# Attention stage of a fused attention, MoE and MLP kernel: router tables in the steps without a conversion, a 16-bit sign operation, local values loaded ready-made, value copies on ScalarE

## The chip, the cores and the metric

The kernel runs on one core of a Trainium2 chip. The metric is the device time of one execution in microseconds, as the median of three runs. The engines are named as in the profile: PE (TensorE matmul), PEld (its weight loads), DVE (VectorE), ACT (ScalarE), POOL (GpSimd), SP (SyncE, which issues the loads and stores here). L12 means line 12 of the kernel before; where the changed kernel is meant, the text says so.

## What is computed

Three layers follow one another. Only the first is touched by the change, apart from tables that the second needs.

```python
def _attn_ref(q, k, v, n_global, n_local):          # (4, 8, 768, 64), 8 global, 96 local
    scores = scale * np.matmul(q, k.transpose(0, 1, 3, 2))
    keep = is_global | is_local                     # 8 first columns, or 96 last ones
    scores = np.where(keep, scores + bias, -1e9)
    a = softmax(scores)
    return np.matmul(a, v)

x = _moe_ref(x, w_gate, w1, w2)                     # 3072 tokens, 8 experts, capacity 384, greedy by logit
return _moe2_ref(x, w_in, w_out, alpha)             # float64 weights w_in, w_out; parametric ReLU
```

The softmax weights, the values and x are fp32. `w_in` and `w_out` arrive as 64-bit floats and are turned into fp32 on the chip, during the attention stage.

## The kernel before

**Attention, lines 90 to 340.** The 3072 rows are 24 tiles of 128 queries (4 batches of 6 tiles, `g`), and each tile is done in two half steps (`u`) of four heads. That makes 48 steps, counted by `n`; `steps[n]` is `(g, u)`. The engines each have a queue in program order, and the order of the code in the loop over `n` is therefore the order of work on each of them. In step `n` the loop issues, in turn: the loads for later tiles (SP), `scores` of step n+1 (eight matmuls on PE, L193; four minimum-and-add operations on DVE, L199, into `a_sx`; four exponentials on ACT, L202, into `a_p`), `transpose_p` of step n (PE, L213; the own block's copy `a_pts0` on DVE, L217; the block of earlier keys `a_pts1` on ACT, L215), `divisor` (POOL, L243), `combine` of step n-2 (PE L261; DVE L247, L270, L280 and at u = 1 L283), and `values` of step n-1 (PE, L232; the copy `a_xt` out of PSUM, L236 on ACT at u = 1 and L238 on DVE at u = 0).

**Values of earlier keys.** A tile that is not the first of its batch looks at 96 local keys of the tile before and at 8 global keys. The kernel before takes them from the tile before as it stands: `place_values` (L173, copy in L177 on POOL) overwrites the first 32 rows of that tile's values with a strip `a_vg`, in which the global values lie beside zeros, once the tile before has used them. The weights `a_p` are 256 columns wide, with zeros in front.

**Conversion of the 64-bit weights, `Doubles`, lines 30 to 87.** There are 32 jobs of 128x512 numbers. In a step with `turn(n)` (`2 <= n < 45` and `n % 5 < 4`, so four steps of five, called turn steps here) one job begins and is joined: `begin` runs two ACT operations (L72, L74) and one on POOL (L73), before the step's scores; `join` runs at the step's end two operations on DVE (L78 shifts, L79 puts the sign bit in) and one on POOL (L81). `finish` of every second job runs two more on POOL (L86, L87) in the next turn step. The raw numbers `f_raw` have three buffers, so the load of job k is issued when L81 of job k-3 is over.

**Router tables, `Router.setup`, from line 465.** Constants for the MoE routing are made by small operations on POOL and DVE. `setup` is a generator that the attention loop steps once in each step from n = 1, whether it is a turn step or not.

After the attention stage comes the routing, whose first search runs with nothing beside it, and then the experts' matmuls, one expert after the other, with the rest of the routing among them.

```python
if turn(n):
    next(side)
if n:
    next(setup, None)
```

## Time and profile before

| | us |
|---|---|
| median of three runs (lowest, highest) | 1077.29 (1076.77, 1078.17) |
| the profiled execution | 1076.5 |
| its span, first to last instruction | 1074.7 |
| busy in the span: PE, DVE, ACT, POOL | 1032.3, 739.1, 380.3, 559.5 |
| mean granted TensorE clock | 0.986 of full speed |

The attention stage is the first 196 us or so of the span; the rest is routing and the experts. The profile's page cuts the span into 40 slices of 26.9 us. The views by stretch, by group, by wait and by time are asked for the attention stage alone, since an average over the whole span says little on it.

### The profile page before, as it was taken

What the parts mean: (1) busy time and instruction counts of PE and PEld (TensorE: products, weight loads), DVE (VectorE), ACT (ScalarE), POOL (GpSimd) and SP (SyncE); (2) the same over time, 40 slices, a digit from 0 to 9 for tenths busy, and PEclk for the clock granted to TensorE, in tenths of its full rate; (3) what the DMA queues carried; (4) which work ended last, traced back from release to release, by engine and by line L of the source; (5) the groups of instructions that cost most, each with busy time, mean ns of one, the idle gap of its engine ahead of it and who ended that gap; (6) DMA issues with size and microseconds to landing.
All of it is one profiled execution on the core that took longest, in us unless ns stands there. A gap on an engine that the chain in (4) does not pass through costs nothing.

```text
span 1074.7 us, 19352 instructions
## 1 busy us (share of the span) xinstructions
PE 1032.3 (96%) x6475; PEld 908.8 (85%) x6475; DVE 739.1 (69%) x2215; ACT 380.3 (35%) x958; POOL 559.5 (52%) x867
## 2 busy tenths in 40 slices
PE   8888989789999999999999999999999999999997
PEld 6766767569888988898899888988998999999996
DVE  7999999787878787877887788678855313231322
ACT  6788878233224311331233123312321232124211
POOL 5867876055668434643564346433742464247223
PEclk9999999799999999999999999999999999999999
DMA  8677774152254336335433643543354335335141
GB/s 287 221 243 262 269 268 156 31 150 77 98 193 151 127 109 215 99 109 175 157 93 106 208 136 98 163 151 119 99 175 139 120 124 189 118 118 167 60 136 70
DMA packets 86771, 160.80 MB, mean 150 GB/s; under 512 B 9584, under 2 KB 42864, under 8 KB 86672
## 3 DMA queue, kind: packets, MB, share of 16 engines
q1 hardware_dynamic: 82832, 146.98, 41.3%
q0 software_dynamic: 3840, 12.59, 3.5%
q8 instruction: 51, 0.84, 0.3%
q14 instruction: 48, 0.39, 0.1%
HBM read 138.57 MB, written 20.97 MB: 148 GB/s over the span
## 4 chain that ended last, share of the span: by engine, by line
PE 74%; DVE 6%; POOL 3%; issue 3%; DMA 1%; ACT 1%; POOLq 0%; DVEq 0%; ACTq 0%
PE m_h L983 22%; PE m_acc L1028 22%; PE m_acc L970 12%; PE m_h L943 11%; POOL m_g L912 1%; PE a_xp L232 1%; PE a_pt L213 1%; POOL m_so L912 1%; PE a_s L193 1%; DMA m_x<-x_rows,r_idx 1%; PE m_h L869 1%; ACT a_p L202 1%; DVE r_red L795 1%; PE a_cb L261 1%; DVE a_sx L199 1%
## 5 line engine op out<-in xcount | busy, mean ns | idle before, releaser
L912 POOL TENSOR_TENSOR m_g<-m_t,m_g 128x192 fp32r<-128x192 f32 (+1 forms) x286 | 163.7, 594 | 335.6 <-ACT m_g L992 335.0
L1028 PE MATMUL m_acc<-m_so,m_g 128*128 128x512 f32 x1143 | 294.0, 398 | 0.0
L983 PE MATMUL m_h<-m_y,wi 128*128 128x384 f32 x1536 | 290.1, 339 | 0.0
L983 PEld LDWEIGHTS m_h<-m_y,wi 128*128 128x128 f32 x1536 | 267.4, 188 | 6.6 <-DVE m_xt L885 0.2
L1028 PEld LDWEIGHTS m_acc<-m_so,m_g 128*128 128x128 f32 x1143 | 209.2, 189 | 34.5 <-POOL m_g L912 0.5
L912 POOL TENSOR_TENSOR m_s<-m_r,m_s 128x256 fp32r<-128x256 f32 x256 | 187.3, 755 | 77.5 <-ACT m_s L902 77.2
L992 ACT ACTIVATE m_g<-m_t 128x384 fp32r<-128x384 f32 (+1 forms) x143 | 70.0, 489 | 427.0 <-DVE m_t L991 249.1
L990 DVE TENSOR_SCALAR m_t<-m_h,m_al 128x384 f32<-128x384 f32 (+1 forms) x144 | 82.3, 571 | 155.7 <-PE m_h L983 145.4
L970 PE MATMUL m_acc<-m_hh,m_s 128*128 128x384 f32 x768 | 148.0, 339 | 0.0
L943 PE MATMUL m_h<-m_xt,m_s 128*128 128x384 f32 x768 | 144.4, 336 | 0.6 <-DVE m_xt L885 0.4
L943 PEld LDWEIGHTS m_h<-m_xt,m_s 128*128 128x128 f32 x768 | 134.5, 188 | 2.4 <-DVE m_xt L885 0.6
L970 PEld LDWEIGHTS m_acc<-m_hh,m_s 128*128 128x128 f32 x768 | 132.7, 189 | 0.0
L902 ACT ACTIVATE m_s<-m_r 128x512 fp32r<-128x512 f32 x128 | 79.7, 626 | 68.4 <-PE m_acc L970 66.7
L202 ACT ACTIVATE a_p<-a_sx,a_mn 128x232 f32<-128x232 f32 (+1 forms) x192 | 88.4, 462 | 38.2 <-DVE a_mn L199 38.2
L947 DVE SCALAR_TENSOR_TENSOR m_hh<-m_h,m_hh 128x384 fp32r<-128x384 f32 x64 | 35.5, 555 | 78.4 <-ACT m_hh L946 78.2
L991 DVE SCALAR_TENSOR_TENSOR m_t<-m_h,m_t 128x384 f32<-128x384 f32 (+1 forms) x144 | 73.9, 513 | 4.9
L795 DVE TENSOR_REDUCE r_red<-r_cmp 128x24 bf16<-128x576 bf16 (+1 forms) x97 | 73.8, 761 | 3.3
L213 PE MATMUL a_pt<-ident,a_p 128*128 128x128 f32 x352 | 57.3, 294 | 15.9 <-DVE a_r L247 13.2
L213 PEld LDWEIGHTS a_pt<-ident,a_p 128*128 128x128 f32 x352 | 39.2, 144 | 36.9 <-ACT a_p L202 23.1
L199 DVE CUSTOM_DVE_ANT_0 a_sx<-a_s,a_bias 128x232 f32<-128x232 f32 (+1 forms) x192 | 61.4, 374 | 4.3 <-PE a_s L193 2.6
L946 ACT ACTIVATE m_hh<-m_h 128x384 fp32r<-128x384 f32 x64 | 31.5, 492 | 91.1 <-PE m_h L943 88.8
L193 PE MATMUL a_s<-a_k,a_q 64*128 64x232 f32 (+1 forms) x384 | 51.0, 388 | 3.6 <-DMA a_q<-in_q_dram 3.6
(192 smaller groups left out, 1162.4 us busy)
## 6 DMA issues: line engine op xcount, KB each, us to landing
m_so<-wo_pairs SPq DMA_DIRECT2D x112, 512.0 KB, 3.5
m_r<-in_moe_w_dram SPq DMA_DIRECT2D x128, 256.0 KB, 3.0
a_k<-in_k_dram SPq DMA_DIRECT2D x20, 464.0 KB, 5.2
f_raw<-in_moe_w_in_dram SPq DMA_DIRECT2D x16, 512.0 KB, 4.0
f_raw<-in_moe_w_out_dram SPq DMA_DIRECT2D x16, 512.0 KB, 5.4
wo_pairs<-m_so SPq DMA_DIRECT2D x16, 512.0 KB, 2.7
a_v<-in_v_dram SPq DMA_DIRECT2D x24, 256.0 KB, 5.1
x_rows<-a_xo SPq DMA_DIRECT2D x24, 256.0 KB, 3.0
```

The source lines that it names most:

```text
L199: nc.vector.tensor_tensor_reduce(out=sx[:, s, :n], in0=ps[s][:, a, :n], in1=bs[:, h], scale=-scale, scalar=BIG, op0=OP.add, op1=OP.min, ac ...
L202: nc.scalar.activation(pr[:, s, 2 * C - n:], sx[:, s, :n], AF.Exp, bias=T["mn", g][:, h:h + 1], scale=-1.0, accum_out=T["sum", g][:, h:h + 1])
L213: nc.tensor.transpose(ps[:, i], pr[:, :C] if part else pr[:, C:], ident)
L795: nc.vector.tensor_reduce(red, cmp, axis=AX.X, op=OP.add)
L902: self.nc.scalar.activation(s[:, 0], r, AF.Copy)
L912: self.nc.gpsimd.tensor_tensor(lo[:, c:c + n], x[:, c:c + n], hi[:, c:c + n], op=OP.subtract)
L943: nc.tensor.matmul(ps[:, :n], s1[:, a, d], x[:, b, d], start=(d == 0 and i == 0), stop=(d == self.ND - 1 and i == 2))
L970: nc.tensor.matmul(ps[:, :n], s2[:, b, d * 128:(d + 1) * 128], h[:, a], start=(f == 0 and a + b == 0), stop=(last and a == 1))
L983: nc.tensor.matmul(ps[:, :n], self.wi[:, a, d, f * 128:(f + 1) * 128], y[:, b, d], start=(d == 0 and i == 0), stop=(d == self.ND - 1 and i ...
L990: nc.vector.tensor_scalar(t[:, cs], ps[:, cs], 0.0, self.al[:, f:f + 1], op0=OP.min, op1=OP.mult)
L991: nc.vector.scalar_tensor_tensor(t[:, cs], ps[:, cs], 0.0, t[:, cs], op0=OP.max, op1=OP.add)
L1028: self.nc.tensor.matmul(self.ex[e]["op"][t], g[:, a, t * 128:(t + 1) * 128], s[:, b], start=(f == 0 and a + b == 0), stop=(f == self.F2 // ...
```

## The change

Five edits, all in the attention stage:

1. `join` no longer puts the sign into the shifted number. It masks the top 16 bits of the high word and writes them into the top 16 bits of the low word's place, which are zero there, and the addition on POOL (L81) then carries the sign along. The operation has one input instead of two, of 16-bit elements that lie 8 bytes apart.
2. The local and global values of earlier keys are laid out in DRAM as an input `vw` of 104 rows per tile, and loaded as a tile `a_vw` with a DMA of its own (20 in all, 104 x 2 KB). `place_values`, `a_vg` and its loads, and two memsets go. `a_v` has three buffers instead of four.
3. The weights are 232 instead of 256 columns wide, and the block of earlier keys is transposed as 104 rows.
4. `a_xt` is copied on ACT in every step.
5. `setup` is stepped only in steps that are not turn steps, and its pieces are cut anew; the two copies that make `r_tp` go from DVE to ACT.

```diff
     def join(self, job):
         nc, t = self.nc, job["t"]
+        parts = job["raw"].bitcast(U16).rearrange("p a (b c) -> p a b c", c=2)
         nc.vector.tensor_scalar(t, t, 3, 0x7FFFFFF8, op0=OP.logical_shift_left, op1=OP.bitwise_and)
-        nc.vector.scalar_tensor_tensor(t, job["raw"][:, :, 1], -0x80000000, t, op0=OP.bitwise_and, op1=OP.bitwise_or)
+        nc.vector.tensor_scalar(parts[:, :, 0, 1], parts[:, :, 1, 1], 0x8000, None, op0=OP.bitwise_and)
...
-        x = T["v", g] = loads.tile([C, H, D], FT, name="a_v", bufs=4)
+        x = T["v", g] = loads.tile([C, H, D], FT, name="a_v", bufs=3)
         nc.sync.dma_start(x, v[b, t * C:(t + 1) * C])
-        if not t:
-            nc.sync.dma_start(vg[C - GW:C - W, b % 2], v[b, :G])
+        if t:
+            x = T["vw", g] = loads.tile([GW, H, D], FT, name="a_vw", bufs=3)
+            nc.sync.dma_start(x, vw[b, t - 1])
...
-    def place_values(g, u):
-        b, t = divmod(g, NT)
-        if t:
-            hs = slice(4 * u, 4 * u + 4)
-            nc.gpsimd.tensor_copy(T["v", g - 1][:C - W, hs], vg[:, b % 2, hs])
...
+        m = GW if part else C
+        ps = psum.tile([C, 4, C], FT, name=f"a_pt{part}")[:m]
+        sb = work.tile([C, 4, C], FT, name=f"a_pts{part}", bufs=2)[:m]
...
-            parts.append((T["v", g - 1], T.pop(("PT", g, u, 1))))
+            parts.append((T["vw", g], T.pop(("PT", g, u, 1))))
...
-        if u:
-            nc.scalar.activation(xt, ps, AF.Copy)
-        else:
-            nc.vector.tensor_copy(xt, ps)
+        nc.scalar.activation(xt, ps, AF.Copy)
...
-        if n + 1 < N:
-            place_values(*steps[n + 1])
         if turn(n):
             next(side)
-        if n:
+        else:
             next(setup, None)
...
-        nc.vector.tensor_copy(self.tp[:, :, 0], first[:, :, None].to_broadcast([128, U, NB, 2]))
-        nc.vector.tensor_copy(self.tp[:, :, 1], inner[:, :, None, None].to_broadcast([128, U, NB, 2]))
+        for k, t in enumerate((first[:, :, None], inner[:, :, None, None])):
+            nc.scalar.activation(self.tp[:, :, k], t.to_broadcast([128, U, NB, 2]), AF.Copy)
```

How the queues change, at three places. First DVE at the end of a turn step with odd n, before the change (`a_pts`, `a_lp`, `a_xo` and `logits` belong to transposition and combination, `f_t` and `f_raw` to the conversion):

```order
L217 COPY a_pts_484<-a_pt_483 128x512 [waits PE_49]
L247 RECIPROCAL a_r<-a_se 128x4 [waits Pool_49]
L270 TENSOR_TENSOR a_lp<-a_cb,a_r 128x32 [waits DVE_49,PE_49]
L280 TENSOR_TENSOR a_xo<-a_cb,a_r 128x256
L283 TENSOR_REDUCE logits<-a_lp 128x8 [waits DVE_49]
L238 COPY a_xt<-a_xp 128x256 [waits PE_49]
L78 TENSOR_SCALAR f_t<-f_t 128x512 [waits Pool_49]
L79 SCALAR_TENSOR_TENSOR f_t<-f_raw,f_t 128x512 [waits DMAHW1_49,DVE_49]
```

The same step in the changed kernel:

```order
L211 COPY a_pts_494<-a_pt_493 128x512 [waits PE_49]
L238 RECIPROCAL a_r<-a_se 128x4 [waits Pool_49]
L261 TENSOR_TENSOR a_lp<-a_cb,a_r 128x32 [waits DVE_49,PE_49]
L271 TENSOR_TENSOR a_xo<-a_cb,a_r 128x256
L274 TENSOR_REDUCE logits<-a_lp 128x8 [waits DVE_49]
L79 TENSOR_SCALAR f_t<-f_t 128x512 [waits Pool_49]
L80 TENSOR_SCALAR f_raw<-f_raw 128x512 [waits DMAHW2_49,Activation_49]
```

The copy of `a_xt` is gone from DVE, and the last operation waits for ACT (L74, which writes the low word's place) instead of for the operation in front of it.

Second, ACT over two turn steps, before:

```order
L202 ACTIVATE a_p,a_sum<-a_sx,a_mn 128x232 x4
L215 ACTIVATE a_pts_631<-a_pt_630 128x512
L72 ACTIVATE f_t<-f_raw 128x512
L74 ACTIVATE f_raw<-f_raw 128x512
L202 ACTIVATE a_p,a_sum<-a_sx,a_mn 128x232 x4
L215 ACTIVATE a_pts_702<-a_pt_701 128x512
L236 ACTIVATE a_xt<-a_xp 128x256
```

And after (each exponential stands in a row of its own there):

```order
L195 ACTIVATE a_p,a_sum<-a_sx,a_mn 128x232 [waits DVE_49,Activation_49]
L209 ACTIVATE a_pts_635<-a_pt_634 104x512 [waits PE_49,Activation_49]
L229 ACTIVATE a_xt<-a_xp 128x256 [waits PE_49,Activation_49]
L72 ACTIVATE f_t<-f_raw 128x512 [waits DMAHW7_49,Pool_49]
L74 ACTIVATE f_raw<-f_raw 128x512
...
L209 ACTIVATE a_pts_696<-a_pt_695 104x512 [waits PE_49,Activation_49]
L229 ACTIVATE a_xt<-a_xp 128x256 [waits PE_49,Activation_49]
```

Now every step has a copy of `a_xt` behind `a_pts` and ahead of the next conversion, and this copy waits for PE's `values`.

Third, POOL over a turn step in which a job is finished, before:

```order
L501 IOTA r_grid 128x52
L501 IOTA r_grid 128x46
L501 IOTA r_grid 128x50
L73 TENSOR_SCALAR f_t<-f_t 128x512
L86 TENSOR_SCALAR wi<-f_t 128x512
L87 TENSOR_TENSOR wi<-f_t,wi 128x512
L243 TENSOR_SCALAR a_se<-a_sum 128x4
L177 COPY a_v<-a_vg 32x256
L81 TENSOR_TENSOR wo<-f_t,f_raw 128x512
```

And after:

```order
L73 TENSOR_SCALAR f_t<-f_t 128x512
L87 TENSOR_SCALAR wi<-f_t 128x512
L88 TENSOR_TENSOR wi<-f_t,wi 128x512
L234 TENSOR_SCALAR a_se<-a_sum 128x4
L82 TENSOR_TENSOR wo<-f_t,f_raw 128x512
```

The tables and the copy into `a_v`, which waits for PE, no longer stand between the conversion's operations. The tables' POOL part stands in steps 0, 1 and 4.

## Rows read from the trace of the kernel before

**Rows 1.** The page, part 2: DVE's busy tenths in 40 slices of 26.9 us.

```profile
DVE  7999999787878787877887788678855313231322
```

**Rows 2.** Busy time by stretch: PE, PEld, DVE, ACT, POOL, granted clock, DMA share, GB/s.

```profile
0.00:20.00 20.00, 16.07 (x112) 11.94 (x112) 15.29 (x77) 11.93 (x44) 8.99 (x26) 1.00 0.85 286
20.00:180.00 160.00, 144.26 (x1344) 112.66 (x1343) 152.44 (x588) 132.22 (x430) 121.38 (x178) 0.97 0.74 249
180.00:200.00 20.00, 18.28 (x203) 14.78 (x201) 17.50 (x76) 12.89 (x48) 5.46 (x13) 1.00 0.12 43
```

**Rows 3.** Waits in 20 to 180 us: us in total, times, longest.

```profile
ACT a_p L202 <- DVE a_mn L199: 27.3, 25, 2.6
...
DVE a_sx L199 <- ACT f_raw L74: 0.7, 1, 0.7
...
DVE a_xt L238 <- PE a_xp L232: 0.4, 2, 0.2
```

**Rows 4.** The chain that ended last, pieces in order: start, length, what.

```profile
120.86 0.39 DVE a_sx L199
...
123.28 0.49 ACT a_pts L215
...
129.72 0.98 PE a_s L193 x8
...
133.24 0.98 PE a_s L193 x8
...
160.60 0.39 DVE a_sx L199
```

**Rows 5.** Timeline of DVE at a turn step's end, odd n: start, duration, instruction.

```profile
104.13 0.42 DVE L238 COPY a_xt<-a_xp 128x256 f32<-128x256 f32 x1
104.46 0.47 DVE L78 TENSOR_SCALAR f_t<-f_t 128x512 int32<-128x512 int32 x1
104.97 0.69 DVE L79 SCALAR_TENSOR_TENSOR f_t<-f_raw,f_t 128x512 int32<-128x512 int32 x1
105.57 0.28 DVE L199 CUSTOM_DVE_ANT_0 a_sx<-a_s,a_bias 128x128 f32<-128x128 f32 x1
```

**Rows 6.** Lines 78 and 79 on DVE: duration ns min/median/max, first and last start.

```profile
L78 DVE TENSOR_SCALAR f_t<-f_t x32: 415/430/1354, 19.9 to 179.0; 128x512 int32<-128x512 int32 x32
...
L79 DVE SCALAR_TENSOR_TENSOR f_t<-f_raw,f_t x32: 691/693/1651, 20.3 to 179.5; 128x512 int32<-128x512 int32 x32
```

**Rows 7.** Timeline of DVE and POOL where two operations meet.

```profile
100.00 1.33 POOL L87 TENSOR_TENSOR wi<-f_t,wi 128x512 fp32r<-128x512 f32 x1
100.23 1.65 DVE L79 SCALAR_TENSOR_TENSOR f_t<-f_raw,f_t 128x512 int32<-128x512 int32 x1
```

**Rows 8.** Timeline of ACT in a stretch without idle time.

```profile
107.46 0.36 ACT L236 ACTIVATE a_xt<-a_xp 128x256 f32<-128x256 f32 x1
107.72 0.66 ACT L72 ACTIVATE f_t<-f_raw 128x512 f32<-128x512 f32 x1
...
108.86 0.47 ACT L202 ACTIVATE a_p<-a_sx,a_mn 128x232 f32<-128x232 f32 x1
...
110.75 0.66 ACT L72 ACTIVATE f_t<-f_raw 128x512 f32<-128x512 f32 x1
```

**Rows 9.** Timeline of DVE: the longest operations of the router tables.

```profile
37.11 1.37 DVE L507 CAST r_tp<-r_first 128x288 bf16<-128x288 f32 x1
...
42.90 1.22 DVE L518 TENSOR_SCALAR r_mask<-r_rows 24x4 bf16<-24x4 int32 x1
...
51.28 1.65 DVE L529 TENSOR_SCALAR r_step<-r_digits 128x72 uint16<-128x72 f32 x2
```

**Rows 10.** Tile `f_raw`: L81's duration (ns min/median/max), and the loads' time to landing.

```profile
L81 POOL TENSOR_TENSOR f_t<-f_t,f_raw x16: 1272/1292/1307, 21.2 to 176.6; 128x512 int32<-128x512 int32 x16
...
DMA to landing us min/median/max: 3.8/4.9/8.2
```

**Rows 11.** Groups on POOL, 0 to 200 us: busy, mean ns, idle before it and its releaser.

```profile
L177 POOL COPY a_v<-a_vg 32x256 f32<-32x256 f32 x40 | 21.5, 538 | 16.6 <-PE a_xp L232 14.6
```

More of the change, by code (lines that the diff above doesn't have):

```diff
@@ L87, in finish, with attention @@
             self.nc.gpsimd.tensor_tensor(job["lo"], v, job["hi"], op=OP.subtract)
-def attention(ctx, tc, q, k0, k, v, w_gate, n_global, n_local, ident, x_dram, logits, side, router):
+def attention(ctx, tc, q, k0, k, v, vw, w_gate, n_global, n_local, ident, x_dram, logits, side, router):
     nc = tc.nc
@@ L208, in transpose_p @@
             return
-        ps = psum.tile([C, 4, C], FT, name=f"a_pt{part}")
-        sb = work.tile([C, 4, C], FT, name=f"a_pts{part}", bufs=2)
+        m = GW if part else C
+        ps = psum.tile([C, 4, C], FT, name=f"a_pt{part}")[:m]
+        sb = work.tile([C, 4, C], FT, name=f"a_pts{part}", bufs=2)[:m]
         for i in range(4):
             pr = T["P", g, 2 * u + i // 2][:, i % 2]
-            nc.tensor.transpose(ps[:, i], pr[:, :C] if part else pr[:, C:], ident)
+            nc.tensor.transpose(ps[:, i], pr[:, :GW] if part else pr[:, GW:], ident)
         if part:
@@ L489, in setup @@
         W, U = self.WIDE, TT // 2
+        ng = 128 // B
+        rows = 2 * NB
         self.slots = iota([128, B // W, TT, W], U16, "r_slots", [[W, B // W], [0, TT], [1, W]])
-        yield
         self.blocks = iota([128, U, NB, 2], U16, "r_blocks", [[0, U], [1, NB], [0, 2]])
-        yield
         first = iota([128, U, 2], FT, "r_first", [[256, U], [128, 2]])
@@ L496, in setup @@
         order = iota([128, E], FT, "r_order", [[-1, E]], base=E)
+        at = iota([rows, ng], I32, "r_rows", [[-1, ng]], base=ng, slope=1)
+        of = iota([rows, 2, NB // ng], I32, "r_cols", [[-NB, 2], [-ng, NB // ng]], base=rows, slope=1)
+        yield
         digits = iota([128, D, TT], FT, "r_digits", [[1, D], [0, TT]], base=1)
         self.last = iota([128, D + 1], FT, "r_last", [[1, D + 1]], base=1)
-        yield
         for (d, size), g in zip(self.HIGH + self.LOW, self.grids):
@@ L530, in setup @@
             self.steps.append(step)
-            if i % 2:
+            if i % 3 == 2:
                 yield
+        yield
         self.ahead = consts.tile([128, 2 * TT], FT, name="r_ahead")
@@ L1151 @@
     v: bass.AP,
+    vw: bass.AP,
     n_global: int,
@@ L1188 @@
         items = [item for both in zip(first, second) for item in both]
-        attention(actx, tc, q, k0, k, v, w_gate, n_global, n_local, ident, x_dram, logits, doubles.jobs(items), router)
+        attention(actx, tc, q, k0, k, v, vw, w_gate, n_global, n_local, ident, x_dram, logits, doubles.jobs(items), router)
         assert doubles.idle
@@ L1216, in _lay_out, with reach @@
     out["k0"] = pairs(k[:, :, None, :c])[:, 0]
-    out["k"] = pairs(np.stack([np.concatenate([k[:, :, :n_global], k[:, :, t * c - n_local:(t + 1) * c]], axis=2)
-                               for t in range(1, s // c)], axis=2))
+    def reach(x, end):
+        return np.stack([np.concatenate([x[:, :, :n_global], x[:, :, t * c - n_local:t * c + end]], axis=2)
+                         for t in range(1, s // c)], axis=2)
+    out["k"] = pairs(reach(k, c))
     out["v"] = inputs["v"].transpose(0, 2, 1, 3)
+    out["vw"] = reach(inputs["v"], 0).transpose(0, 2, 3, 1, 4)
     return out
```

15 lines of the change are left out of this document (3 added, 12 removed).

## The prediction

> **What bounds the kernel now.** I began with the page's busy tenths: DVE is near full in the first seven slices, the attention stage, and at seven to eight tenths after them [rows 1]. All edits lie in that stage, so I asked for busy time by stretch. From 20 to 180 us DVE is busy 152.44 of 160 us, PE 144.26, ACT 132.22 and POOL 121.38 [rows 2]. A busy PE is partly modelled, so I checked by the waits who is waiting: DVE has four entries in that stretch, from 0.7 to 0.4 us in total each, 2.2 us together, while ACT alone waits 27.3 us for DVE's minimum [rows 3]. DVE sets the pace; what it is spared is time, until another engine's queue is as long. What follows the stage depends on its end and is not edited, so it moves with it.
>
> The unit to count in is five steps, four turn steps with a conversion and one without. On the chain the first `a_sx` of a step starts on DVE at 120.86 and, ten steps later, at 160.60 [rows 4]: 39.74 us, **19.87 us per five steps**. The 32 jobs make eight such units.
>
> **What DVE is spared.** Operations on it overlap their neighbours a little, so I count from start to start.
>
> - Copy of `a_xt`: 104.46 - 104.13 = 0.33 us [rows 5]. It is on DVE in every second step, 2.5 per unit: 0.83 us. (The copies before the first and after the last job, 3 of 24, I count at nothing: DVE is not full there, 17.50 of 20 us in the last stretch [rows 2].)
> - Sign bit: L78 takes 0.43 us in the median and L79 0.69 [rows 6]. In rows 5 L78 is followed by L79 0.04 us after its end, since L79 reads what L78 writes, while L79's successor starts 0.09 before L79 ends. So the pair costs now 0.43 + 0.04 + 0.69 - 0.09 = 1.07 us. The new operation has one input in SBUF and 512 elements, as L78 has, and does not read L78's result. If it runs like L78, the pair costs 2 x (0.43 - 0.09) = 0.68 us and each turn step is spared 0.39, which I round to 0.36, for the odd spacing of its elements: 1.44 us per unit. The other bound is that it streams one element per tick as L79 does: 0.69, and then only the dependency is saved, 0.13 us per turn step, 0.26 less than at the first bound. No row has a 16-bit operation of this size. I take the value near L78, the row most alike in operands. The Trainium skill (VectorE: DVE Perf Modes, What auto-detection actually checks) would give it to the new operation on the same grounds: a single source and the destination in SBUF with even dimensions suffice for two elements a tick, and no spacing is asked for. L78's 415 ns, under the 533 ns of 512 ticks at the clock stated there, agrees for closely packed elements; no run here shows spaced ones.
> - Router tables: three entries of 1.37, 1.22 and 1.65 us [rows 9] stand at the end of turn steps, less 0.08 overlap each: 4.0 us in all. The first goes to ACT; the others go to steps without a conversion, which have room for them (below). The smaller ones I leave out.
>
> By DVE alone a unit would fall to 19.87 - 0.83 - 1.44 = **17.6 us**.
>
> **What the other engines allow.** PE: between two starts of `a_s` with no gap lie 133.24 - 129.72 = 3.52 us [rows 4], so five steps take at least 17.6 us. ACT: four exponentials take 110.75 - 108.86 = 1.89 us, the conversion's two operations 108.86 - 107.72 = 1.14, a copy of `a_xt` 107.72 - 107.46 = 0.26 [rows 8], `a_pts1` 0.49 [rows 4]. With the copy in every step a turn step has 3.78 us of ACT work and the fifth 2.64: 17.8 us per unit. So three queues of 17.6 to 17.8 us meet, in different rhythms: ACT is the longest in turn steps (3.78), PE in the fifth (3.52 against 2.64). Some of each rhythm is lost at the others. POOL has the room: it loses 40 copies, 21.5 us, and the 14.6 us in which it stood waiting for PE in front of them [rows 11]. But POOL and DVE go on getting in each other's way: beside a POOL operation that began 0.23 us earlier, L79 took 1.65 instead of 0.69 us [rows 7], and the longest L78 1.35 instead of 0.43 [rows 6]. These waits are in the 19.87 and I leave them in. I take **18.1 us** per unit, 0.3 above ACT's sum.
>
> **New waits.** The sign operation now waits for L74 on ACT, behind which all of DVE's next step is queued. L74 runs before the step's exponentials, some two microseconds ahead: nothing, and if the raw numbers came late, DVE would wait anyway for L78's input. The copy of `a_xt` on ACT waits for PE's `values`; the conversion and the next exponentials are queued behind it. At u = 1 it stands there already. SP gets 20 more issues, each with 104 x 2 KB = 213 KB, 4.3 MB in all, and is rid of four small ones. Some 18 of them fall between 20 and 180 us; that adds 3.8 MB in 160 us, 24 GB/s, to 249, and the shorter unit makes (249 + 24) x 19.87 / 18.1 = 300 of it; in proportion the DMA share goes from 0.74 to 0.89. The first 20 us ran 286 GB/s at 0.85 [rows 2], so this fits, with little to spare. Two of the new loads stand ahead of the first raw numbers: 0.5 us. Transposing 104 instead of 128 rows and the narrower weights change no column count on PE: nothing. The two memsets that go: nothing, since POOL was busy for only 8.99 of the first 20 us [rows 2].
>
> **The sum.** Eight units: 8 x (19.87 - 18.1) = 14.2 us. Tables: 4.0, of which 1.0 is lost because ACT's 3.78 us fill those steps instead: 3.0. First loads: -0.5. Together 16.7 us. The profiled execution took 1076.5 us (span 1074.7 and 1.8 around it), so 1059.8; the median of the three runs is 0.8 higher, so **1060.5 us**.
>
> **Rivals.**
>
> *A, the sign operation is no cheaper.* Either it streams one element per tick, or it loses its gain to POOL. The second is to be taken seriously: two operations of L78's kind then stand one behind the other, and a POOL operation that gets in between makes the second wait as in rows 7, at up to 0.96 us. The Trainium skill (SBUF — State Buffer, Who interferes with whom) has the rule: the two share a port pair, and who comes second waits for the whole instruction. Rows 7 agree. DVE's unit is then 17.6 + 4 x 0.26 = 18.64, with little lost at the others 18.84: 8 x 1.03 + 2.5 = 10.7 us gained, 1066.6 us. Chance 0.2.
>
> *B, the queues mesh and the POOL waits shrink*, as the copies into `a_v` no longer delay L81 and what follows. The unit falls to ACT's 17.8, and the tables count in full: 8 x 2.07 + 4.0 = 20.6 us, 1056.7 us; with PE's sum 1055. For it: ACT's 27.3 us of waiting show that it can run ahead. Against: nothing here has three full queues. Chance 0.15.
>
> *C, ACT becomes the gate.* If the copy of `a_xt` waits for PE's last work of a step in each step, the 1.14 us of the conversion come after it and no longer beside PE's work. Where half of it, 0.57 us in four steps, is lost on top of 17.8, the unit is 20.1, and only the tables are gained: 1077.3 - 2.5 + 1.8 = 1076.6 us. Against: the exponentials run a step ahead of their transposition, and at u = 1 the order is the same today without any such wait among the long ones. Chance 0.09.
>
> *D, slower: the raw numbers come late.* Load of job k starts when L81 of job k-3 ends. From the start of L72 to the end of L81 it is about one step, 3.97 us, L81's 1.29 [rows 10] and some 0.6 between: 5.9 us. Three jobs thus take at least landing + 5.9, a unit 4/3 of it. With the median landing of 4.9 us [rows 10] that is 14.4 us, no bound. It decides from a landing of 9.0 us on (19.87); today's longest is 8.2. At 11 us, where the fuller DMA engines would have to push it, the unit is 22.5: 8 x 2.66 - 2.5 = 19 us lost, 1096 us. For it: a share of 0.89. Against: the median is far off, and the loads issued per step are limited, so that no backlog builds up. Chance 0.06.
>
> **How the numbers follow.** The forecast has 0.5, with 1057 to 1064 for units of 17.8 to 18.5 us; A reaches to 1070 and B to 1053. 1053 to 1070 leaves out D, C and the ends of A and B, some 0.2. A measurement tells apart about 0.2%, 2.2 us. Faster: the forecast, A, B and the half of C in which less is lost at ACT, 0.9; within 0.2% the rest of C, 0.04; slower D, 0.06.
>
> **What would show it.** In the changed profile: the stage's last `a_xp` some 17 us earlier; 18.1 us per five steps; DVE's busy share from 20 to 160 us below 0.95 with waits for PE or ACT among its first; L80 near 0.43 us in the median; the 27.3 us in which ACT waits for DVE shrunk to under a third; DMA near 300 GB/s with landings under 7 us. A median of 0.69 for L80, or a sum of its waits above 8 us, means A; ACT's doubles waiting for a DMA means D. I am wrong in kind, not in size, if DVE is still without waits and the unit is above 19 us.

## The result, and the profile after

The changed kernel takes **1064.43 us** (median of five runs, 1063.83 to 1066.32) against 1076.77 us of the kernel before in five runs on the same chip: a ratio of 0.9885, 95% interval 0.9871 to 0.9898. So 12.3 us are gained, where 16.7 were forecast. The profiled execution took 1064.5 us, its span 1062.8. The gain lies in the attention stage: the last `a_xp` on PE starts at 184.3 us instead of 195.7, 11.4 us earlier where 17 were forecast, and what follows takes as long as before (878.5 against 879.0 us). From here on line numbers are those of the changed kernel: L79 is the shift, L80 the new sign operation, L82 the addition on POOL, L88 its subtraction in `finish`, L192 the score reduction, L195 the exponentials, L229 the copy `a_xt`.

Busy time by stretch, of the changed kernel: stretch, its length, PE, PEld, DVE, ACT, POOL with their instructions, granted clock, DMA share, GB/s [answers to rows 2].

```profile
0.00:20.00 20.00, 14.03 (x96) 10.74 (x98) 13.19 (x70) 10.81 (x39) 7.40 (x26) 1.00 0.90 289
20.00:160.00 140.00, 133.07 (x1280) 102.90 (x1276) 133.59 (x542) 129.88 (x432) 102.26 (x134) 1.00 0.90 298
20.00:180.00 160.00, 152.54 (x1467) 118.18 (x1464) 151.57 (x613) 146.76 (x490) 112.41 (x148) 1.00 0.84 278
```

ACT and PE have come up to DVE: from 20 to 160 us the three are busy 129.88, 133.07 and 133.59 of 140 us. DVE itself is about as busy as before: 151.57 of 160 us, where rows 2 have 152.44. The waits, 20 to 180 us: us in total, times, longest [answers to rows 3].

```profile
POOL f_t L82 <- DVE f_raw L80: 15.3, 12, 1.7
...
ACT a_p L195 <- DVE a_mn L192: 11.4, 15, 1.6
...
DVE a_sx L192 <- PE a_s L186: 2.7, 3, 1.2
...
DVE f_t L79 <- POOL f_t L73: 0.7, 1, 0.7
```

DVE waits 3.8 us in 160, in four entries of which the two longest are shown; that is about as little as before (2.2), so it is still the bound. What it does with its time is seen in the two operations of `join`: first the duration in ns (min/median/max) and first and last start, then the groups with busy time and mean ns, of the changed kernel [answers to rows 6].

```profile
L79 DVE TENSOR_SCALAR f_t<-f_t x32: 410/419/1355, 21.0 to 167.6; 128x512 int32<-128x512 int32 x32
...
L80 DVE TENSOR_SCALAR f_raw<-f_raw x32: 737/750/1835, 21.3 to 168.0; 128x512 uint16<-128x512 uint16 x32
...
L80 DVE TENSOR_SCALAR f_raw<-f_raw 128x512 uint16<-128x512 uint16 x32 | 34.0, 1064 | 0.0
...
L79 DVE TENSOR_SCALAR f_t<-f_t 128x512 int32<-128x512 int32 x32 | 16.5, 517 | 0.8 <-POOL f_t L73 0.7
```

The same groups of the kernel before, where L79 is the old sign operation and L78 the shift:

```profile
L79 DVE SCALAR_TENSOR_TENSOR f_t<-f_raw,f_t 128x512 int32<-128x512 int32 x32 | 26.6, 832 | 1.1
L78 DVE TENSOR_SCALAR f_t<-f_t 128x512 int32<-128x512 int32 x32 | 19.2, 599 | 0.6 <-POOL f_t L73 0.5
```

The new sign operation takes 0.750 us in the median, not 0.43, and not even the 0.693 of the old one [rows 6]; its mean is 1.064. The mean of the pair went up, from 599 + 832 = 1431 ns to 517 + 1064 = 1581. Two places on DVE's timeline show the two cases (start, duration, instruction):

```profile
110.69 0.42 DVE L79 TENSOR_SCALAR f_t<-f_t 128x512 int32<-128x512 int32 x1
111.02 1.82 DVE L80 TENSOR_SCALAR f_raw<-f_raw 128x512 uint16<-128x512 uint16 x1
112.64 0.41 DVE L192 CUSTOM_DVE_ANT_0 a_sx<-a_s,a_bias 128x232 f32<-128x232 f32 x1
...
115.25 0.42 DVE L79 TENSOR_SCALAR f_t<-f_t 128x512 int32<-128x512 int32 x1
115.58 0.75 DVE L80 TENSOR_SCALAR f_raw<-f_raw 128x512 uint16<-128x512 uint16 x1
116.11 0.42 DVE L192 CUSTOM_DVE_ANT_0 a_sx<-a_s,a_bias 128x232 f32<-128x232 f32 x1
...
150.51 0.42 DVE L192 CUSTOM_DVE_ANT_0 a_sx<-a_s,a_bias 128x232 f32<-128x232 f32 x1
```

And POOL's at the first of them:

```profile
110.84 1.40 POOL L88 TENSOR_TENSOR wi<-f_t,wi 128x512 fp32r<-128x512 f32 x1
```

Undisturbed, the pair costs 116.11 - 115.25 = 0.86 us from start to start, where the prediction had 1.07 before and 0.68 after: 0.21 us saved, not 0.36. L80, begun at 111.02, takes 1.82 us: POOL's L88, begun while L79 ran, is over at 112.24, and L80 ends 0.60 us after that. Nine of the 32 sign operations are of that kind, all in steps with a `finish`. One more (1.16 us) and four shifts (0.91 to 1.35 us) meet operations of a `finish` too, so that 14 of its 16 turns cost the pair time.

In the kernel before, 13 of 16 did, so the meetings are not more frequent now; they are longer. There POOL's subtraction (L87) had mostly begun ahead of the shift, which then lost only what was left of it:

```profile
118.66 1.27 POOL L87 TENSOR_TENSOR wi<-f_t,wi 128x512 fp32r<-128x512 f32 x1
118.88 1.33 DVE L78 TENSOR_SCALAR f_t<-f_t 128x512 int32<-128x512 int32 x1
120.25 0.69 DVE L79 SCALAR_TENSOR_TENSOR f_t<-f_raw,f_t 128x512 int32<-128x512 int32 x1
```

Of the subtractions that met the pair, eight began ahead of the shift before the change and four behind its start; in the changed kernel it is four and nine.

The unit of five steps comes from the first and the last L192 that end a pair there, ten steps apart (n = 28 to 38, as in rows 4): (150.51 - 112.64) / 2 = **18.93 us**, against 19.87 before and 18.1 forecast. From the first score reduction of step 13 to that of step 43 (52.11 to 164.94 us; before 56.78 to 176.40) it is 18.81 against 19.94. The loads of the raw numbers, tile `f_raw`, time to landing [answers to rows 10]:

```profile
DMA to landing us min/median/max: 5.0/7.8/8.0
```

### The profile page after: what moved, and what is told of

Its sections match the earlier page's. It is cut to its first block, busy times and chain, and to the rows that moved or that the text cites. A ratio compares the mean times of both kernels' runs of the same rounds, so it can differ in the third digit from the quotient of the medians.

```text
span 1062.8 us, 19360 instructions
## 1 busy us (share of the span) xinstructions
PE 1027.4 (97%) x6475; PEld 904.7 (85%) x6475; DVE 725.7 (68%) x2189; ACT 386.4 (36%) x984; POOL 544.0 (51%) x825
## 4 chain that ended last, share of the span: by engine, by line
PE 79%; DVE 8%; POOL 4%; issue 3%; ACT 3%; DMA 2%; SPq 0%; POOLq 0%; ACTq 0%; DVEq 0%
PE m_h L969 23%; PE m_acc L1014 23%; PE m_acc L956 12%; PE m_h L929 12%; PE a_pt L207 2%; PE a_xp L226 2%; PE a_s L186 2%; ACT a_p L195 2%; DVE f_raw L80 1%; POOL m_so L898 1%; POOL m_g L898 1%; PE a_cb L252 1%; DVE a_sx L192 1%; PE m_h L855 1%; DMA f_raw<-in_moe_w_out_dram 1%
## 5 line engine op out<-in xcount | busy, mean ns | idle before, releaser
L195 ACT ACTIVATE a_p<-a_sx,a_mn 128x232 f32<-128x232 f32 (+1 forms) x192 | 88.4, 466 | 19.5 <-DVE a_mn L192 19.3
L192 DVE CUSTOM_DVE_ANT_0 a_sx<-a_s,a_bias 128x232 f32<-128x232 f32 (+1 forms) x192 | 62.4, 381 | 7.2 <-PE a_s L186 7.0
L207 PE MATMUL a_pt<-ident,a_p 128*128 128x128 f32 (+1 forms) x352 | 57.8, 289 | 6.9 <-DVE a_r L238 3.2
L207 PEld LDWEIGHTS a_pt<-ident,a_p 128*128 128x128 f32 (+1 forms) x352 | 37.6, 137 | 28.8 <-ACT a_p L195 15.2
```

The costliest lines, as they stand in the source:

```text
L192: nc.vector.tensor_tensor_reduce(out=sx[:, s, :n], in0=ps[s][:, a, :n], in1=bs[:, h], scale=-scale, scalar=BIG, op0=OP.add, op1=OP.min, ac ...
L195: nc.scalar.activation(pr[:, s, KW - n:], sx[:, s, :n], AF.Exp, bias=T["mn", g][:, h:h + 1], scale=-1.0, accum_out=T["sum", g][:, h:h + 1])
L207: nc.tensor.transpose(ps[:, i], pr[:, :GW] if part else pr[:, GW:], ident)
```

## The experiments

All times are medians of five executions unless said otherwise; ratios are to the kernel before on the same chip. Differences to the changed kernel, such as "4.0 us", compare medians from separate sets of runs; taken by what each kernel gains on the one before in its own set, they come out up to 1.0 us otherwise (4.5 in experiment 1, 7.8 in 2, 0.5 in 3, 3.7 in 4, 7.2 in 11).

**1. The old sign operation put back** into the changed kernel.

```diff
...
-        nc.vector.tensor_scalar(parts[:, :, 0, 1], parts[:, :, 1, 1], 0x8000, None, op0=OP.bitwise_and)
+        nc.vector.scalar_tensor_tensor(t, job["raw"][:, :, 1], -0x80000000, t, op0=OP.bitwise_and, op1=OP.bitwise_or)
```

> The changed kernel with edit 1 undone: the sign bit goes in by the old operation with two inputs. Theory S (the sign operation): in the changed profile it takes 0.75 us in the median and not 0.43, so the pair on DVE costs 0.34 + 0.66 = 1.00 us a turn step against 1.07 before; DVE is still the bound, and edit 1 is worth 32 x 0.07 = 2 us and no more. Expected: 1066 to 1067 us. Theory O (others): ACT, PE or the DMA engines already hold the changed kernel, so that DVE's price for the sign does not count: 1064 to 1065 us. If edit 1 were worth the 11.5 us that the prediction gave it: 1075 us.

1068.42 us, ratio 0.9928 [0.9914, 0.9941]. Edit 1 is worth 4.0 us: far from the 8 x 1.44 = 11.5 us of the prediction, but somewhat more than expected here. The unit over the same steps is 19.33, so 8 x 0.40 = 3.2 us of it lie in the units. The old operation's mean is 969 ns in this setting and the shift's 486, above medians of 693 and 417, so POOL cost the pair time with the old form as well: nine of the subtractions began behind the shift's start, as in the changed kernel.

**2. The signs left out**: edit 1's operation removed, nothing in its place.

```diff
-        nc.vector.tensor_scalar(parts[:, :, 0, 1], parts[:, :, 1, 1], 0x8000, None, op0=OP.bitwise_and)
```

> The changed kernel without any sign operation: the signs of the converted weights are left out of the computation. Theory S: DVE is spared 0.66 us a turn step and the waits of the sign operation for POOL, on average 1.06 - 0.75 = 0.31 us, so 4 x 0.97 = 3.9 us per five steps, more than it takes to reach the next bounds (17.6 to 17.8 us per five steps against 18.93 now): 8 x (18.93 - 18.1) = 6.6 up to 9 us gained, 1055 to 1058 us. Theory O: at most 2 us gained, 1062 us or more.

1056.05 us, ratio 0.9811 [0.9796, 0.9825]. So 8.4 us hang on the 34.0 us of sign operations; then another limit is met. Busy time by stretch:

```profile
20.00:160.00 140.00, 137.47 (x1360) 109.78 (x1359) 122.31 (x543) 137.89 (x462) 103.73 (x143) 1.00 0.95 313
```

DVE has room (122.31 of 140), ACT and PE are full (137.89 and 137.47). The unit, taken over the same steps, is 17.83 us, beside the 17.8 that the prediction worked out for ACT. That they agree is partly luck: the prediction added up steps of full width, but eight of the 48 (a batch's first tile, without earlier keys) have no `a_pts1` and exponentials of 128 instead of 232 columns. From step 13 to step 43 (49.42 to 154.22 us) the unit of this kernel is 17.47.

**3. Only three of the twenty loads of `a_vw`**, later tiles use those again.

```diff
-            x = T["vw", g] = loads.tile([GW, H, D], FT, name="a_vw", bufs=3)
-            nc.sync.dma_start(x, vw[b, t - 1])
+            i = len(seen)
+            seen.append(g)
+            if i < 3:
+                vws.append(loads.tile([GW, H, D], FT, name=f"a_vw{i}", bufs=1))
+                nc.sync.dma_start(vws[i], vw[b, t - 1])
+            T["vw", g] = vws[i % 3]
```

> The changed kernel with three loads of local values instead of twenty: the strips of the first three tiles stand in for those of all others. It takes 3.5 MB out of the DMA engines, whose share from 20 to 160 us is 0.90 in the changed profile, with a median landing of 7.8 us for the raw numbers. Theory S: ACT waits for raw numbers for only 2.2 us in all, so at most 1.5 us are gained: 1063 to 1064.5 us. Theory O in the form that the DMA engines hold the stage: 4 us or more gained, 1060 us or less.

1063.42 us, ratio 0.9891 [0.9877, 0.9905]: 1.0 us, no more than the runs differ among themselves (1062.72 to 1067.31). The raw numbers' median landing falls from 7.8 to 4.4 us and the DMA share from 0.90 to 0.82, and the unit stays at 18.95. So the fuller queues cost 1 us at most.

**4. The copy `a_xt` back on DVE at u = 0.**

```diff
-        nc.scalar.activation(xt, ps, AF.Copy)
+        if u:
+            nc.scalar.activation(xt, ps, AF.Copy)
+        else:
+            nc.vector.tensor_copy(xt, ps)
```

> The changed kernel with edit 4 undone: in every second step the copy of the values is on DVE again. Theory S: DVE is the bound, the copy costs it 0.33 us in 2.5 steps of five, 8 x 0.83 = 6.6 us lost: 1070 to 1071 us. Theory O in the form that ACT holds the stage: 1065 us or less.

1067.57 us, ratio 0.9921 [0.9908, 0.9935]: 3.1 us, between the two theories. The groups of this kernel suggest why:

```profile
L80 DVE TENSOR_SCALAR f_raw<-f_raw 128x512 uint16<-128x512 uint16 x32 | 27.6, 863 | 0.0
L79 DVE TENSOR_SCALAR f_t<-f_t 128x512 int32<-128x512 int32 x32 | 20.1, 629 | 0.7 <-POOL f_t L73 0.6
```

I count as time lost to POOL what the means lie above the medians (750 and 424 ns here). With `a_xt` on DVE that is 32 x (113 + 205) = 10.2 us, in the changed kernel 32 x (314 + 98) = 13.2 us. So the copy costs its 6.6 us on DVE, and 3.0 of them come back as less time lost to POOL: 3.6, near the 3.1 measured. The number of meetings is no smaller (13 of 16); but with the copy in front of it the shift starts later, and nine of the subtractions have begun ahead of it.

**5. What the form of the operation costs**, a single run: a bench in front of the attention stage (it alone makes this run 1165.6 us long), each form twice with POOL idle, then three times beside POOL subtractions of L88's form.

```diff
...
+            for _ in range(n):
+                v.tensor_scalar(parts[:, :, 0, 1], parts[:, :, 1, 1], 0x8000, None, op0=M)
+            for _ in range(n):
+                v.tensor_scalar(halves[:, 0], parts[:, :, 1, 1], 0x8000, None, op0=M)
+            for _ in range(n):
+                v.tensor_scalar(parts[:, :, 0, 1], halves[:, 0], 0x8000, None, op0=M)
+            for _ in range(n):
+                v.tensor_scalar(halves[:, 1], halves[:, 0], 0x8000, None, op0=M)
+            for _ in range(n):
+                v.tensor_scalar(raw[:, :, 0], raw[:, :, 1], -0x80000000, None, op0=M)
...
+            for _ in range(n):
+                v.tensor_scalar(two[:, :, 0], two[:, :, 1], 0x8000, None, op0=M)
```

> The changed kernel with a stretch put in front that measures the disputed operation by itself on DVE: nine forms of 512 elements, first with POOL idle, then beside a row of POOL subtractions of 512 elements (1.3 us each). With POOL idle, theory S expects 0.42 us for L79's form (packed 32-bit) and 0.75 us for the 16-bit form of L80. What makes it slow is open: if it is the spaced reading, the form with spaced input and packed output takes 0.75 and the one with packed input and spaced output 0.42 or less; if it is the writing of half words, the other way round; if the operation simply runs one element a tick, all spaced forms take 0.6 to 0.7 and do not wait for POOL in the second part. The 32-bit form with spaced input and output, which masks the sign as well, is the candidate for a cheaper one: 0.42 if spacing costs nothing. Beside POOL, forms that share its port are expected to take up to 1.3 us more, the others the same as without.

DVE's timeline (start, us for the group, instruction and count). The lines are, in order: 16-bit, 8 bytes apart in and out (the changed kernel's form); 8 bytes apart in, packed out; packed in, 8 bytes apart out; packed; 32-bit, 8 bytes apart in and out; 16-bit, 4 bytes apart in and out; and the first of them again beside POOL.

```profile
6.31 1.49 DVE L1161 TENSOR_SCALAR b_raw<-b_raw 128x512 uint16<-128x512 uint16 x2
7.60 0.92 DVE L1163 TENSOR_SCALAR b_half<-b_raw 128x512 uint16<-128x512 uint16 x2
8.55 1.50 DVE L1165 TENSOR_SCALAR b_raw<-b_half 128x512 uint16<-128x512 uint16 x2
9.85 0.65 DVE L1167 TENSOR_SCALAR b_half<-b_half 128x512 uint16<-128x512 uint16 x2
10.41 0.88 DVE L1169 TENSOR_SCALAR b_raw<-b_raw 128x512 int32<-128x512 int32 x2
...
12.00 0.93 DVE L1173 TENSOR_SCALAR b_flat<-b_flat 128x512 uint16<-128x512 uint16 x2
...
17.57 4.92 DVE L1161 TENSOR_SCALAR b_raw<-b_raw 128x512 uint16<-128x512 uint16 x3
```

Neither the spacing alone (0.44 us for each of the 32-bit pair) nor the reading of half words 8 bytes apart (0.46) is dear; **writing half words 8 bytes apart** is: 0.745 us. Four bytes apart they take 0.465. And beside POOL the form pays like the others: 1.64 us each, 0.9 more than alone, where the others pay 0.6 to 1.0 more.

**6. The sign made by POOL** in place of DVE, by a comparison and a product, with the same half words written.

```diff
-        nc.vector.tensor_scalar(parts[:, :, 0, 1], parts[:, :, 1, 1], 0x8000, None, op0=OP.bitwise_and)
+        nc.gpsimd.tensor_scalar(parts[:, :, 0, 1], job["raw"][:, :, 1], 0.0, 32768.0, op0=OP.is_lt, op1=OP.mult)
```

> The changed kernel with the sign operation on POOL instead of DVE (comparison of the high word with zero, times 32768). Theory S: DVE is spared as in the run without it, 3.9 us per five steps, and POOL, which is busy 102 of 140 us from 20 to 160 us, takes 32 x 0.62 us more and begins L82 earlier: 1056 to 1059 us, near the run with the signs left out. Theory P: POOL's chain of a finishing turn step (L73 0.61, L87 0.63, L88 1.34, a_se 0.4, sign 0.6, L82 1.3, together 4.9 us) becomes the bound in every second turn step and delays L79: 1062 us or more.

1114.85 us, ratio 1.0369 [1.0355, 1.0383]. The groups of this kernel show why (busy us, mean ns):

```profile
L80 POOL TENSOR_SCALAR f_raw<-f_raw 128x512 uint16<-128x512 int32 x28 | 75.6, 2701 | 2.2
```

I had priced it like POOL's other operations of this size; it takes 2.70 us, where L73 with packed 32-bit elements takes 0.61. POOL becomes the gate, as theory P had it, only far more. The run says nothing on DVE. Nor does it show that the half words are what is dear on POOL, for the operation and the spacing of what it reads differ from L73's too.

**7. The router tables alone** (edit 5 put into the kernel before).

```diff
-        if n:
+        else:
             next(setup, None)
...
-            if i % 2:
+            if i % 3 == 2:
                 yield
```

> The kernel before with edit 5 alone (router tables in steps without a conversion, two copies on ACT). The prediction gave it 3 to 4 us: 1072 to 1073.5 us. If the other engines swallow it: 1076 us. If the smaller table operations and the shorter POOL queue count too: up to 6 us, 1070 us.

1071.16 us against 1076.01, ratio 0.9959 [0.9946, 0.9973]: 4.9 us, where the prediction had 3.0. Not all of it need be the tables' price. The kernel before, in its profiled execution, has three places where the granted clock of TensorE is low (busy time by stretch, clock third from the end):

```profile
40.00:60.00 20.00, 17.09 (x152) 13.41 (x154) 19.15 (x75) 15.53 (x53) 13.33 (x21) 0.91 0.67 213
60.00:80.00 20.00, 17.87 (x157) 13.68 (x155) 19.31 (x79) 15.86 (x54) 14.68 (x22) 0.91 0.77 268
160.00:180.00 20.00, 18.26 (x166) 14.88 (x163) 18.48 (x73) 16.53 (x54) 14.32 (x22) 0.91 0.66 215
```

It is at 0.50 there, 1.2 instead of 2.4 GHz, from about 41 to 44, 64 to 68 and 164 to 167 us, each time soon after PE had stood idle for DVE (2.03, 2.09 and 1.59 us). On the chain that ended last, the same four transpositions then take 1.11 instead of 0.66 us:

```profile
143.53 0.66 PE a_pt L213 x4
...
163.57 1.11 PE a_pt L213 x4
```

With the tables moved, the clock is 1.00 from 20 to 180 us, as it is in the changed kernel, although PE stands idle 1.61 us once there too. Of the 6.0 us by which the stage ends earlier in this run's profile, 3.7 lie in steps 8 to 13 (from score reduction to score reduction), with the long table operations and the first of these places; 0.85 and 0.75 lie in the five steps with each of the other two, the last of which has no tables; and 1.1 lie ahead of step 3. How the 4.9 us divide between the tables and the clock no run shows.

**8. The values of earlier keys alone** (edits 2 and 3 put into the kernel before).

```diff
...
-        if not t:
-            nc.sync.dma_start(vg[C - GW:C - W, b % 2], v[b, :G])
+        if t:
+            x = T["vw", g] = loads.tile([GW, H, D], FT, name="a_vw", bufs=3)
+            nc.sync.dma_start(x, vw[b, t - 1])
```

> The kernel before with edits 2 and 3 alone (local values loaded ready-made, narrower weights). The prediction gave them a loss of 0.5 us: 1076 to 1077 us. If the POOL copies that go had held the conversion up (waits of L78 and L79 for POOL, loads of raw numbers released earlier), 2 to 4 us gained: 1072 to 1074 us. If the 4.3 MB more delay the stage: 1078 us or more.

1074.94 us against 1076.01, ratio 0.9991 [0.9982, 1.0]: 1 us or nothing, between the two expected, though POOL is rid of its 40 copies [rows 11].

**9. The sign as a 32-bit operation.** ACT's low part goes into the low half of the high word; DVE keeps sign and low half with one AND in place.

```diff
-        nc.scalar.activation(raw[:, :, 0], raw[:, :, 0].bitcast(U32), AF.Copy, scale=2.0 ** -29)
+        low = raw.bitcast(U16).rearrange("p a (b c) -> p a b c", c=2)[:, :, 1, 0]
+        nc.scalar.activation(low, raw[:, :, 0].bitcast(U32), AF.Copy, scale=2.0 ** -29)
...
-        nc.vector.tensor_scalar(parts[:, :, 0, 1], parts[:, :, 1, 1], 0x8000, None, op0=OP.bitwise_and)
+        nc.vector.tensor_scalar(job["raw"][:, :, 1], job["raw"][:, :, 1], -0x7FFF0001, None, op0=OP.bitwise_and)
...
-        nc.gpsimd.tensor_tensor(dst, t, job["raw"][:, :, 0], op=OP.add)
+        nc.gpsimd.tensor_tensor(dst, t, job["raw"][:, :, 1], op=OP.add)
```

> The sign as one 32-bit operation: ScalarE (L74 before) writes its 16-bit low part into the low half of the high word, which its first operation has read by then, and VectorE keeps sign and low half with one 32-bit AND in place, 8 bytes apart, a form that took 0.44 us with GpSimd idle; the half-word form takes 0.745 us. Theory F (VectorE's chain sets the turn step, so the form of the sign operation counts): the operation falls from 0.745 to about 0.44 us, 32 x 0.3 = 9.8 us, of which ScalarE and TensorE at 17.8 us a unit let pass what lies above 1056: 1056 to 1060 us, the unit at 17.8 to 18.2 us. Theory G (GpSimd's order sets the step: it slips its subtraction in before the sign operation, whatever the form): the mean of the operation falls by less than 0.15 us, 1062 to 1065 us. Theory H (16-bit writes 8 bytes apart cost ScalarE as they cost the other two engines): its 0.68 us operation goes to 1 us or more, ScalarE sets the step, 1064 us or more.

1072.32 us (nine executions), ratio 0.9967 [0.9957, 0.9978]: theory H. Duration on DVE and on ACT (ns min/median/max; L75 is ACT's second operation):

```profile
L80 DVE TENSOR_SCALAR f_raw<-f_raw x32: 413/426/1489, 20.1 to 174.0; 128x512 int32<-128x512 int32 x32
```

```profile
L75 ACT ACTIVATE f_raw<-f_raw x32: 1359/1366/1376, 18.5 to 172.5; 128x512 uint16<-128x512 uint32 x32
```

DVE's operation is as cheap as hoped, but the half words, 8 bytes apart, have only been handed to ACT, which writes them in 1.37 us instead of 0.68. ACT is then busy 138.76 of the 140 us and waits for others 0.3.

**10. The sign operation earlier**: unchanged, but behind the four score reductions of its step, so that L88 can't get in behind the shift.

```diff
+    def sign(self, job):
...
+        nc.vector.tensor_scalar(parts[:, :, 0, 1], parts[:, :, 1, 1], 0x8000, None, op0=OP.bitwise_and)
...
-        nc.vector.tensor_scalar(parts[:, :, 0, 1], parts[:, :, 1, 1], 0x8000, None, op0=OP.bitwise_and)
...
             if nx:
                 scores(*nx)
+            if turn(n):
+                next(side)
```

> The 16-bit sign operation unchanged, but put on VectorE behind the four score reductions of its turn step instead of behind the shift at the step's end, so that GpSimd's subtraction of the job before can't begin between the two. Theory F2 (about 10 of 32 sign operations take 1.82 us instead of 0.75 because that subtraction slips in, and that is lost time on the bound): sum of the sign operations' waits falls from 10.2 us to under 4 us and the shift's stay near 3 us: 1056 to 1060 us. Theory G2 (the subtraction meets some other VectorE operation in whatever place, or the sign operation now waits for ScalarE's low part): waits only move, 1062 to 1066 us.

1065.31 us (four executions), ratio 0.9901 [0.9887, 0.9915]: nothing gained, theory G2. The groups (L83 is the sign, L87 the shift here):

```profile
L83 DVE TENSOR_SCALAR f_raw<-f_raw 128x512 uint16<-128x512 uint16 x32 | 28.5, 890 | 3.5 <-ACT f_raw L78 3.2
...
L87 DVE TENSOR_SCALAR f_t<-f_t 128x512 int32<-128x512 int32 x32 | 19.5, 610 | 2.3 <-POOL f_t L77 2.3
```

The sign's mean falls from 1064 to 890 ns, the shift's rises from 517 to 610, and DVE now waits 3.2 us for ACT's low part and 2.3 for POOL. The time lost moves rather than ends.

**11. The half words written 4 bytes apart.** ACT writes its low part, 32-bit as in the changed kernel, into a packed tile of its own, and DVE puts the sign into that.

```diff
-        nc.scalar.activation(raw[:, :, 0], raw[:, :, 0].bitcast(U32), AF.Copy, scale=2.0 ** -29)
+        low = job["low"] = self.pool.tile([128, self.WIDTH], I32, name="f64_low", bufs=3)
+        nc.scalar.activation(low, raw[:, :, 0].bitcast(U32), AF.Copy, scale=2.0 ** -29)
...
-        nc.vector.tensor_scalar(parts[:, :, 0, 1], parts[:, :, 1, 1], 0x8000, None, op0=OP.bitwise_and)
+        nc.vector.tensor_scalar(job["low"].bitcast(U16).rearrange("p (a c) -> p a c", c=2)[:, :, 1],
+                                job["raw"].bitcast(U16).rearrange("p a (b c) -> p a b c", c=2)[:, :, 1, 1],
+                                0x8000, None, op0=OP.bitwise_and)
...
-        nc.gpsimd.tensor_tensor(dst, t, job["raw"][:, :, 0], op=OP.add)
+        nc.gpsimd.tensor_tensor(dst, t, job["low"], op=OP.add)
```

> ScalarE writes its low part (32-bit, as before) into a tile of its own, packed, so that the sign's half words are written 4 bytes apart instead of 8; half words written 4 bytes apart took 0.465 us with GpSimd idle, 8 bytes apart 0.745 us, and ScalarE keeps its 0.68 us. Nothing else changes: this is the change as the prediction had priced it (a sign operation at about 0.43 us). Theory F (the form of the sign operation is what the forecast lacked): median of the sign operation near 0.47 us, its mean near 0.8 us, 32 x 0.28 = 9 us of VectorE's chain, stopped by ScalarE and TensorE at 17.8 us a unit: 1057 to 1060.5 us, unit 17.8 to 18.2 us. Theory G (what is saved in the operation is lost to GpSimd's port or to ScalarE at the step's end): 1062 to 1065 us, unit 18.6 us or more.

**1056.19 us** (1056.08 to 1057.03), ratio 0.9818 [0.9804, 0.9831]: faster than both kernels, 0.8 us below theory F's range, and as fast as the one of experiment 2 that makes no sign at all. Duration, then the groups (busy us, mean ns), then busy time by stretch:

```profile
L80 DVE TENSOR_SCALAR f_low<-f_raw x32: 441/462/1558, 19.7 to 160.9; 128x512 uint16<-128x512 uint16 x32
```

```profile
L80 DVE TENSOR_SCALAR f_low<-f_raw 128x512 uint16<-128x512 uint16 x32 | 22.7, 709 | 0.0
L75 ACT ACTIVATE f_low<-f_raw 128x512 int32<-128x512 uint32 x32 | 21.8, 682 | 0.0
L79 DVE TENSOR_SCALAR f_t<-f_t 128x512 int32<-128x512 int32 x32 | 18.2, 569 | 0.8 <-POOL f_t L73 0.7
```

```profile
20.00:160.00 140.00, 135.51 (x1324) 106.56 (x1323) 132.24 (x562) 135.12 (x449) 101.37 (x139) 1.00 0.93 310
```

The median falls from 0.750 to 0.462 us, 32 x 0.29 = 9.2 us, and 8.2 us come out (7.2 by what each gains on the kernel before). The time lost to POOL, counted as in experiment 4, is 32 x (247 + 151) = 12.7 us, about the 13.2 of the changed kernel, and 14 of 16 turns of `finish` meet the pair as there: what this kernel saves is the form's price, not time lost to POOL. The unit is 17.97 us.

**12. Experiment 11 with `a_xt` back on DVE at u = 0**, the edit of experiment 4.

```diff
-        nc.scalar.activation(xt, ps, AF.Copy)
+        if u:
+            nc.scalar.activation(xt, ps, AF.Copy)
+        else:
+            nc.vector.tensor_copy(xt, ps)
```

> The packed low part kept, and the value copy of the u = 0 steps back on VectorE as in the kernel before. Theory V (VectorE's chain still sets the unit): it gets 0.33 us x 2.5 = 0.83 us a unit back, 8 x 0.83 = 6.6 us, less the few us that came of giving the copy back without the packed form (3.1 us): 1059.5 to 1063 us, unit 18.4 us or more. Theory W (ScalarE and TensorE, busy 135.1 and 135.5 of the 140 us from 20 to 160 us, are the gate now, and VectorE has room): 1054 to 1058 us, unit 17.6 to 18.1 us.

1059.92 us, ratio 0.9845 [0.9831, 0.9858]: theory V by the time, 3.7 us lost; the unit is 18.33, just under its 18.4. Though three engines are nearly full, DVE's share still counts, again for about half of the copy's 6.6 us, and again the time lost to POOL falls, from 12.7 to 32 x (112 + 186) = 9.5 us.

## Why the prediction was right, and where it was not

The forecast of 1060.5 us lay 3.9 us below the measured 1064.4. The time is just outside what the forecast gave itself (1057 to 1064) and inside the range only because that reached out for rival A. The units missed by 6.7 us, and a larger gain than forecast at the tables hid 1.9 of that, which is luck. Step by step:

- **The bound.** Right. DVE sets the pace in both kernels, and what it is spared is time: experiments 1, 2, 4, 11 and 12 change DVE's work first of all, and each moves the total. But the forecast wanted DVE's share from 20 to 160 us below 0.95, with waits among its first; it is 0.954 (133.59 of 140), with 3.8 us of waits in the longer stretch. The prediction would have called itself wrong in kind if DVE had no waits and the unit were above 19 us: the first all but came true, the second, at 18.93, just not.
- **The sign operation: the step that failed.** The prediction put 0.43 us, "the value near L78, the row most alike in operands", and took off 0.36 us per turn step, 11.5 us in all. Measured: 0.75 us alone, 0.86 us for the pair from start to start. That is 0.21 us per turn step, 6.7 us in all. From this goes what POOL adds: counted as in experiment 4 but with the old form in place (experiment 1's means of 969 and 486 ns over its medians of 693 and 417) it is 32 x (276 + 69) = 11.0 us, with the new form 13.2. 6.7 - 2.2 = 4.5 us, beside the 4.0 to 4.5 measured. The operands were alike in number, place and length, but not in the spacing of what is written. The upper bound of 0.69 was too low as well. Experiment 11 gives the operation nearly the price that the prediction had assumed (0.46 us), and takes 8.2 us less.
- By the Trainium skill (VectorE: DVE Perf Modes, What auto-detection actually checks) the spacing should not have mattered: a single source and even dimensions in SBUF would do for two elements a tick. Experiment 5 disagrees for half words written 8 bytes apart (0.745 us against 0.44 for 32-bit elements with the same spacing); the measurement decides.
- **Rival A** described most of what happened: a sign operation no cheaper, with a POOL operation getting between the two of `join`, and a unit of 18.84 us (measured 18.93). Its first branch weighs most, since experiment 11 gains its 8.2 us with as much time lost to POOL. Its sign, a sum of L80's waits above 8 us, is met: 32 x (1064 - 750) = 10.0 us. Its 1066.6 us is 2.2 above the measured time; it used 2.5 us for the tables, and edit 5 brought 4.9 alone. The rule cited with it, the Trainium skill (SBUF — State Buffer, Who interferes with whom), agrees with the trace here: L80, begun at 111.02 while L88 ran, ended only at 112.84, after L88's end at 112.24.
- **The copy `a_xt`.** 6.6 us on DVE by rows, 3.1 and 3.7 us when undone (experiments 4 and 12). The prediction left POOL's intrusions "in the 19.87" as a constant; they are not. In the kernel before they are 32 x (139 + 169) = 9.9 us, and 13.2 in the changed one, in 13 and 14 meetings with `finish`. The order at the step's end goes with them: without the copy the shift is mostly ahead of POOL's subtraction, and the operation behind it loses about 1 us; with the copy (the kernel before, experiments 4 and 12) the subtraction is mostly ahead.
- **The tables.** 3.0 forecast, 4.9 measured alone. The prediction left out the smaller entries, and it had no term for the granted clock: the kernel before has three places at 1.2 GHz in the stage's profile and the changed kernel none (experiment 7). Which of these made the difference stays open, and so does whether 1.0 us was lost to ACT.
- **The new loads.** -0.5 forecast. Alone, with the copies on POOL gone, they bring about 1 us (experiment 8), and leaving most of them out brings nothing (experiment 3). The 0.5 us itself no run shows, since the start differs from run to run: the first score reduction of step 3 starts at 15.14 us in the profiled execution of the changed kernel and at 13.70 before, but between 12.68 and 13.85 in experiments 1 to 4 and 9 to 12, which start with the same loads. The DMA share of 0.89 and 300 GB/s were forecast, and 0.90 and 298 came from 20 to 160 us; landings "under 7 us" did not: 7.8 in the median. Nothing follows from that, since rival D needed 9.0.
- **The floor.** Over steps 28 to 38 the unit came down to 17.83 us in experiment 2 and 17.97 in experiment 11, where 17.8 was ACT's sum and 18.1 was taken. But the sum counts steps of full width only, and over more steps experiment 2 lies below it (17.47). ACT's wait for DVE fell from 27.3 to 11.4 us, to 0.42 and not under a third; in experiment 9, where ACT was given more, it is gone, and the time is 7.9 us longer than that of the changed kernel, which is how a gate at ACT (rival C) looks.
- **The sum.** 8 x (19.87 - 18.93) = 7.5 us from the units and 4.9 from the tables make 12.4, and 12.3 were measured. That close an agreement is chance: the profiles have 12.9 us between step 3 and step 43, 4.9 of them in steps 8 to 13, and 1.4 lost ahead of step 3, while the edits by themselves add up to 4.0 (edit 1), 3.1 (edit 4), 4.9 (edit 5) and 1.1 (edits 2 and 3), 13.1 us. Against the forecast's 16.7, 6.7 were missing in the units and 1.9 more came from the tables.

What stays open: that the order of shift and subtraction causes the extra time lost is read from the traces of six kernels, and no experiment set that order by itself or took POOL's `finish` away. What the low clock cost the kernel before is not measured either.

## What to carry to other kernels

Price an operation by a row of the same element width and the same spacing on the side that is *written*; number of operands and elements is not enough. When an engine is full and meets another one, a saving on it need not come back whole: the copy's 6.6 us came back at about half, as the order of two operations changed and with it what each meeting cost, while 8.2 of the packed form's 9.2 us came back. So add up the time lost (mean over median, times the number) in both kernels, and look which of the two operations began first. And when a cost is handed from one engine to another, look whether it is the layout that costs: a packed tile in between removed it, where moving the work to ACT or POOL made it dearer. Last, compare the granted clock stretch by stretch before a gain is put down to one edit.
